# Re-timing six steps in a hand-ordered attention and feed-forward kernel: hash, turns, norm, means and loads

## The chip, the cores and the metric

The kernel runs on one core of one Trainium2 chip. The metric is device microseconds of one execution; of several runs the median is told. Engines are named as the profile names them: PE is TensorE (PEld its weight loads), DVE is VectorE, ACT is ScalarE, POOL is GpSimd and SP is SyncE, which here only issues DMAs.

## The reference

Inputs are q, k and v (4 batches, 8 heads, 768 tokens, 64 dims), a projection to 6 hash bits, and the weights of a gated feed-forward layer.

```
q_bucket, k_bucket = bits of (q @ proj > 0), (k @ proj > 0), read as numbers
scores = (q @ k.T) / 8, and -1e9 where the buckets differ
attn   = softmax(scores) @ v                       # per batch and head
x      = attn as [4 * 768 tokens, 8 * 64]
xn     = x / sqrt(mean(x * x) + 1e-6) * rms_g
out    = (silu(xn @ w_gate) * (xn @ w_val)) @ w_out    # 512 -> 1536 -> 512
```

## The kernel before, in words

The tokens are worked on in eight windows w of 384 queries: batch b = w // 2, half w % 2. A window has 8 heads, in 4 pairs hp. The attention of one head against all 768 keys is three slots, p = 0, 1, 2; a slot is one pair of score products (`scores`, L344) into one PSUM tile and one exponential on ACT over it (`probs`, L354). The mask is part of the score product: q and k carry 12 further rows of hash bits below their 64 dims, so the tile `QK` has 76 rows. Value products (`av`, L366) come two and three slots behind the head's last slot, in two halves of nine.

All order is written out by hand. `plan[s]` holds the steps of slot s, put there by `at(s, step, ..., rank=)`. The main loop takes slot after slot: first `scores(s + 1)`, then the steps of rank under 3, then `probs(s + 1)`, then the rest by rank. Each engine executes its instructions in this order, so a step that waits holds back all that stands behind it on the same engine.

The pieces that the change touches:

- Turns. In batch 0 and in the first pair of batch 1, q and k are turned on PE: `keep_pair(b, hp, i)` makes three transposes into a PSUM bank `t_ps` (L170) and has DVE copy them to `kT` or `qT` (L178), for i = 0 to 3: k and q of the pair's first head, then of its second. `casts` brings the copy to fp16 in `QK`, mostly on POOL (L186), one half in batch 0 on ACT (L184). In the other pairs DVE turns the blocks itself (`turn_dve`, L194, four steps for k and four for q) straight from the loaded tile, and POOL casts (L202).
- Hashes. `hash_one`, `hash_pair`, `hash_lone`, `hash_pairs` compute four fp32 products into `d_ps` (L210), DVE turns them to `bits` (L217), and copies on DVE (L250, L270) or DMAs on SP's queue (L248, L268, L285, L303) move the 12 rows each to where they belong in `QK`. `hash_lone` and the later form of `hash_pair` issue eight such DMAs.
- Means. `v_mean` multiplies by ones (L325, a bank `m_ps`) and DVE scales it to `cvb` (L328), which `attn_out` adds.
- Output of a pair: `attn_out` on DVE (L381, L386), POOL (L390) and the squares on POOL (L402); the last pair of window 0 is on DVE alone (L390, L397). `sumsq` (L406) reduces the squares on DVE.
- The norm: `norm` (L413 on DVE, L415 and L419 on POOL), `scale_x` (L424 on DVE, one of three chunks), `turn_x` (four transposes on PE, L431, and one product on DVE, L432, into `xnT`). Then the feed-forward block of the window starts: `gate` (L446, tanh on ACT L448), `value` (L456, on DVE L457 and L458) and `project` (L469, copied out on ACT L476 and stored through SP L478). For window w it starts at slot s0 = 24 w + 42. All these small products share three PSUM banks (`bank`), in the order of program and release.
- Loads. `load_rows` (L112) and `load_blocks` (L122, four DMAs) go to SP's queue; weights (`load_w`, `load_wo`) go to POOL's. SP issues in order, and it uses eight completion semaphores in turn, so a DMA waits until the eighth one before it has landed.

The slots run through the pairs in this order, six slots to a line, window 0 and 1 first:

```python
TURNS = [(0, 0), (1, 0), (0, 1), (0, 2), (0, 3), (1, 1), (1, 2), (1, 3)]
TURNS += [(w + 2, hp) for w, hp in TURNS]
SLOTS = [(w, 2 * hp + hh, p) for w, hp in TURNS for hh in range(2) for p in range(3)]
SLOTS += [(w, h, p) for w in range(4, 8) for h in range(H) for p in range(3)]
```

So window 0's last head ends in slot 29, pair 0 of batch 1 is first used in slot 48, pair 1 in 60, pair 2 in 66 and pair 3 in 72.

Of the kernel before, what the change touches and what calls it, by code (L numbers as in the profile page):

```python
# [37 lines left out]
LAST = {(w, h): g for g, (w, h, p) in enumerate(SLOTS) if p == 2}  # L38
# [6 lines left out]
def kernel(  # L45
# [530 lines left out]
    def at(s, f, *a, rank=3):  # L576
        plan[s].append((rank, len(plan[s]), lambda: f(*a)))
# [17 lines left out]
        at(1 + h, cast_half, 0, h, "q", 1)  # L595
        at(h, (bits0, bits1)[h], (nc.vector,), 3)

    for hp, turns, sv in ((1, (1, 2, 4, 5), 8), (2, (7, 8, 9, 10), 17), (3, (12, 13, 14, 15), 22)):
        for i, s in enumerate(turns):
            at(s, keep_pair, 0, hp, i)  # L600
            at(s + 1, casts, 0, hp, i)
        at(sv, v_prep, 0, hp)

    for h, s in ((2, 3), (3, 7)):
        at(s, hash_one, h)
        for t in range(3):
            at(s + 1 + t, lambda h=h, t=t: moves[h]((nc.vector,), t), rank=5)
    for hp, s, slots in ((2, 12, (13, 14, 15, 16)), (3, 17, (18, 19, 20, 21))):
        at(s, hash_pair, 0, hp)
        for i, s in enumerate(slots):  # L610
            at(s, lambda hp=hp, i=i: moves[0, hp](nc.vector, [divmod(i, 2)]), rank=5)
    for hp, s in enumerate((6, 16, 22, 29)):
        at(s, v_mean, 0, hp, 2, range(6))
    for i, (t, src) in enumerate(((wg, moe_w_gate), (wv, moe_w_val))):
        at(2 + 4 * i, load_w, t, src, 0, 768)
# [3 lines left out]

    for which, sl in zip("kqv", (9, 11, 15)):  # L620
        at(sl, load_rows, nc.sync, 1, 0, which)
    for i, sl in enumerate((23, 25, 27, 29)):
        at(sl, keep_pair, 1, 0, i)
        at(sl + 1, casts, 1, 0, i)
    at(31, hash_pair, 1, 0)
    at(27, v_prep, 1, 0)
    for h in range(2):
        at(41 + h, cast_half, 1, h, "q", 0)
# [4 lines left out]
    def in_row(loads, s, hash_slot=None):  # L633
        return loads, range(s, s + 8), (s + 4, s + 8, s + 9), hash_slot

    work = {
        (1, 1): in_row((21, 22, 32), 42, 51), (1, 2): in_row((32, 33, 37), 49, 58),
        (1, 3): in_row((38, 40, 44), 56, 65),
        (2, 0): in_row((53, 55, 58), 64), (2, 1): in_row((59, 62, 66), 72, 81),
        (2, 2): in_row((68, 71, 75), 81), (2, 3): in_row((78, 82, 86), 89, 98),  # L640
        (3, 0): in_row((90, 94, 98), 100), (3, 1): in_row((100, 104, 108), 110, 119),
        (3, 2): in_row((116, 120, 124), 126), (3, 3): in_row((126, 130, 134), 136, 145),
    }
    for (b, hp), (loads, turns, cast_slots, sh) in work.items():
# [12 lines left out]
        at(cast_slots[2], v_sum, b, hp)  # L657
        if b > 1 and hp % 2:
            at(48 * b + (17 if hp == 3 else -4), v_mean, b, hp - 1, 4)
    for hp, s in enumerate((48, 62, 69, 78)):  # L660
        at(s, v_mean, 1, hp, 2)

    gts, sqs = {}, {}
# [13 lines left out]

    for w in range(8):
        for h in range(H):
            end = LAST[w, h] + 3  # L680
            at(end - 1, av, w, h, 0, 9)
            at(end, av, w, h, 9, 18)
            if h % 2:
                at(end, o_step, w, h // 2, rank=4.5)
                if (w, h) != (0, 7):
                    late = 3 if h == 7 and w < 3 else 5 if (w, h) == (0, 5) else 4
                    at(end + late, s_step, w, h // 2, rank=5 if late != 5 else 4)
        s0 = 24 * w + 42
        n0 = {0: 9, 2: 7}.get(w, 11)
        at(s0 - n0, norm, w, rank=5)  # L690
        for c in range(3):
            at(s0 - {0: 5 - c // 2, 2: 6 - c}.get(w, 8 - c), scale_x, w, c, rank=5)
            xs = {0: (3, 2, 1), 2: (4, 2, 1)}.get(w, (5, 3, 1))
            at(s0 - xs[c], turn_x, w, c, rank=1)
        seen = set()
        for ft in range(NF):
            for f, s in ((g_step, s0 + 16 * ft // NF), (v_step, s0 + (32 * ft + 16) // (2 * NF))):
                at(s, f, w, ft, rank=4 if s in seen else 2)
                seen.add(s)
        for i in range(9 if w < 7 else 6):  # L700
            c, j = divmod(i, 3)
            at(s0 + 16 + i, project, w, c, 4 * j, 4 * j + 4, rank=1 if i == 8 else 3)
# [61 lines left out]
```

## Time and profile before

| | us |
|---|---|
| median of 3 runs | 336.01 (335.22 to 336.15) |
| the profiled execution | 334.87 |
| its span, first to last instruction | 333.1 |
| PE busy | 324.1 (97%) |
| DVE busy | 237.9 (71%) |
| ACT busy | 207.8 (62%) |
| POOL busy | 155.6 (47%) |
| mean granted PE clock | 0.999 |

The profile is of one execution; the time of that execution is 1.8 us above its span. In its views a row "start, length, engine, line, operation, out<-in, count" may merge several instructions, and the bracket behind it is the idle time of the engine ahead of it and what ended that wait. Of the chain of waits each row is start, length and what the chain went through.

### The profile page before, as it was taken

Reading aid. Unit: us, or ns where it says so; the run is one execution under the profiler, and the core shown is the slowest. Engines: PE = TensorE matmul, PEld = TensorE weight load, DVE = VectorE, ACT = ScalarE, POOL = GpSimd, SP = SyncE. Lnnn points to the kernel's source line nnn. Section 1 sums busy time; section 2 is a strip of 40 time slices with the busy share of each in tenths; the row PEclk is TensorE's granted clock in tenths of the full one; section 3 lists DMA queues with packets and bytes.
Section 4 is the critical chain, followed back from the end, with each engine's and each line's share of the span. In section 5 each row is a group of like instructions: output and inputs, shape, how many; then the busy total and the mean of one; then the engine's idle time right before and its main releaser. Section 6 shows DMA issues by size and latency. Waiting matters only on the chain.

```text
span 333.1 us, 7797 instructions
## 1 busy us (share of the span) xinstructions
PE 324.1 (97%) x2983; PEld 199.3 (60%) x2983; DVE 237.9 (71%) x532; ACT 207.8 (62%) x324; POOL 155.6 (47%) x230
## 2 busy tenths in 40 slices
PE   8999989999989999999999999999999999999995
PEld 6566666555556556565566656566666656655653
DVE  4789669998588976789577785967357753793860
ACT  3789887665566666657576766657666766422421
POOL 5888955587666665737644364643110311130000
PEclk9999999999999999999999999999999999999999
DMA  7999999887649528308240751000100001002002
GB/s 218 355 229 207 159 138 147 146 143 104 138 83 171 100 49 213 46 18 153 102 81 15 147 128 63 3 16 4 65 33 0 3 31 65 2 1 83 13 0 94
DMA packets 85972, 31.36 MB, mean 94 GB/s; under 512 B 71480, under 2 KB 82992, under 8 KB 85936
## 3 DMA queue, kind: packets, MB, share of 16 engines
q1 hardware_dynamic: 82000, 26.09, 34.3%
q0 software_dynamic: 3712, 4.72, 8.8%
q8 instruction: 23, 0.38, 0.5%
q14 instruction: 13, 0.11, 0.1%
q10 hardware_dynamic: 224, 0.07, 0.1%
HBM read 28.32 MB, written 6.29 MB: 104 GB/s over the span
## 4 chain that ended last, share of the span: by engine, by line
PE 83%; DVE 7%; DMA 4%; POOL 2%; ACT 1%; issue 1%; SPq 0%; DVEq 0%; POOLq 0%; ACTq 0%
PE y_ps L469 18%; PE v_ps L456 16%; PE s_ps L344 15%; PE g_ps L446 14%; PE o_ps L366 8%; PE d_ps L210 4%; PE s_ps L446 4%; DMA wo<-in_moe_w_out_dram 2%; DMA QK<-bits 2%; PE x_ps L431 1%; PE t_ps L170 1%; PE z_ps L337 1%; PE y_ps L721 1%; DVE t L457 1%; DVE otmp L381 1%
## 5 line engine op out<-in xcount | busy, mean ns | idle before, releaser
L354 ACT ACTIVATE psb<-s_ps 128x768 f16<-128x768 f32 x192 | 150.6, 809 | 29.6 <-PE s_ps L344 27.9
L344 PE MATMUL s_ps<-QK 76*128 76x384 f16 x384 | 93.6, 325 | 2.2 <-ACT psb L354 0.9
L456 PE MATMUL v_ps<-xnT,wv 128*128 128x384 f16 x384 | 78.1, 326 | 0.0
L469 PE MATMUL y_ps<-wo,ht 128*128 128x512 f16 x276 | 69.4, 379 | 0.1
L448 ACT ACTIVATE t<-g_ps 128x384 f32<-128x384 f32 x78 | 38.2, 490 | 46.3 <-PE g_ps L446 45.7
L366 PEld LDWEIGHTS <-psb 128*128 128x128 f16 x1152 | 52.2, 97 | 21.8 <-issue 3.7
L457 DVE SCALAR_TENSOR_TENSOR t<-t,g_ps 128x384 f32<-128x384 f32 x78 | 42.7, 547 | 31.0 <-ACT t L448 30.4
L446 PE MATMUL g_ps<-xnT,wg 128*128 128x384 f16 x312 | 63.4, 325 | 1.2 <-DVE xnT L432 0.6
L390 POOL TENSOR_TENSOR x<-otmp,rcp 128x384 f32<-128x384 f32 x31 | 25.9, 835 | 79.3 <-DVE rcp L386 78.8
L458 DVE SCALAR_TENSOR_TENSOR ht<-t,v_ps 128x384 f16<-128x384 f32 x96 | 53.2, 554 | 10.5 <-PE v_ps L456 1.1
L366 PE MATMUL o_ps<-vl,psb 128*128 128x65 f16 x1152 | 56.7, 193 | 0.0
L446 PEld LDWEIGHTS <-wg 128*128 128x128 f16 x384 | 36.0, 97 | 25.1 <-issue 1.7
L456 PEld LDWEIGHTS <-wv 128*128 128x128 f16 x384 | 36.2, 97 | 23.4 <-issue 0.3
L344 PEld LDWEIGHTS <-QK 76*128 76x128 f16 x384 | 31.4, 98 | 19.9 <-issue 6.8
L469 PEld LDWEIGHTS <-ht 128*128 128x128 f16 x276 | 25.8, 97 | 25.1 <-issue 1.6
L476 ACT COPY ysb<-y_ps 128x512 f32<-128x512 f32 x23 | 13.5, 586 | 25.3 <-PE y_ps L469 24.9
L402 POOL TENSOR_TENSOR sq<-x 128x384 f32<-128x384 f32 x31 | 25.7, 828 | 2.5
L202 POOL CAST QK<-qT 64x768 f16<-64x768 f32 x22 | 18.2, 827 | 18.0 <-DVE qT L194 17.3
L432 DVE TENSOR_TENSOR xnT<-x_ps,gcol 128x512 f16<-128x512 f16 x24 | 16.2, 681 | 14.2 <-PE x_ps L431 14.2
L381 DVE TENSOR_TENSOR otmp<-o_ps,cvb 128x390 f32<-128x390 f32 x32 | 17.9, 558 | 8.2 <-PE o_ps L366 8.1
L202 POOL CAST QK<-kT 64x768 f16<-64x768 f32 x22 | 18.2, 828 | 10.5 <-PE v_ps L456 4.0
L194 DVE STREAM_TRANSPOSE kT<-kL 128x192 f32<-128x192 f32 x44 | 22.1, 517 | 0.0
(80 smaller groups left out, 300.0 us busy)
## 6 DMA issues: line engine op xcount, KB each, us to landing
vL<-in_v_dram SPq DMA_DIRECT2D x16, 384.0 KB
out_dram<-ysb SPq DMA_DIRECT2D x23, 256.0 KB
kL<-in_k_dram SPq DMA_DIRECT2D x44, 96.0 KB
qL<-in_q_dram SPq DMA_DIRECT2D x44, 96.0 KB
kL<-in_k_dram SPq DMA_DIRECT2D x4, 384.0 KB
qL<-in_q_dram SPq DMA_DIRECT2D x4, 384.0 KB
wg<-in_moe_w_gate_dram POOLq DMA_DIRECT2D x2, 768.0 KB, 8.6
wv<-in_moe_w_val_dram POOLq DMA_DIRECT2D x2, 768.0 KB, 9.1
```

The lines of the kernel that those rows point to most:

```text
L202: nc.gpsimd.tensor_copy(QK[b, hp][0:64, hh, o : o + S], T0[b, hp, which][64 * hh : 64 * hh + 64, :])
L344: nc.tensor.matmul(ps[:, j, 0:HALF], k_cols(w // 2, h, 2 * p + j), q_cols(w, h), start=True, stop=True,)
L354: nc.scalar.activation(psb[w, h][:, p], sps.pop(g)[:, :, 0:HALF], AF.Exp, scale=ESCALE,)
L366: nc.tensor.matmul(o[:, c, hh, 0:65], psb[w, h][:, jt // 2, jt % 2, 128 * c : 128 * c + 128], vls[b % 2][:, h, v_chunk(b, h, jt), 0:65], s ...
L390: eng.tensor_mul(xd.rearrange("p c (h d) -> p c h d", h=2), tmp[:, :, :, 0:64], r.to_broadcast([128, 3, 2, 64]),)
L402: nc.gpsimd.tensor_mul(sq, xd, xd)
L446: nc.tensor.matmul(g, wg[:, kt, fs], xnT[w][:, kt], start=(kt == 0), stop=(kt == 3))
L448: nc.scalar.activation(t, g, AF.Tanh, scale=0.5)
L456: nc.tensor.matmul(vv, wv[:, kt, fs], xnT[w][:, kt], start=(kt == 0), stop=(kt == 3))
L457: nc.vector.scalar_tensor_tensor(out=t, in0=t, scalar=1.0, in1=g, op0=ALU.add, op1=ALU.mult)
L458: nc.vector.scalar_tensor_tensor(out=ht[w][:, ft], in0=t, scalar=0.5, in1=vv, op0=ALU.mult, op1=ALU.mult)
L469: nc.tensor.matmul(y, ht[w][:, ft, c * 128 : (c + 1) * 128], wo[:, ft, :], start=(ft == 0), stop=(ft == NF - 1),)
```

## The change

Six kinds of steps get other slots; no instruction is added or taken away.

- The turn of head 3's k goes from slot 4 to 3, its casts from 5 to 4; the hash of head 2 from slot 3 to 4, and its three DVE moves one slot on each.
- The mean of pair 3 of batch 0 goes from slot 29 to 30, those of pairs 1 and 2 of batch 1 from 62 to 60 and from 69 to 64.
- The four turns of batch 1's first pair go from slots 23, 25, 27, 29 to 20, 21, 24, 27, the casts with them; its hash from 31 to 33.
- Loads: k and q of (1, 2) from 32 and 33 to 34 and 35; v of (2, 0) from 58 to 59; k, q, v of (2, 1) from 59, 62, 66 to 66, 67, 68; of (2, 2) from 68, 71, 75 to 71, 74, 77.
- The value products of window 0's last head, and with them its output step, go one slot sooner, from 31 and 32 to 30 and 31.
- Window 0's norm goes from slot 33 to 31, its three scalings from 37, 37, 38 to 36, its three turns from 39, 40, 41 to 38, 39, 40.

```diff
-    for hp, turns, sv in ((1, (1, 2, 4, 5), 8), (2, (7, 8, 9, 10), 17), (3, (12, 13, 14, 15), 22)):
+    for hp, turns, sv in ((1, (1, 2, 3, 5), 8), (2, (7, 8, 9, 10), 17), (3, (12, 13, 14, 15), 22)):
...
-    for h, s in ((2, 3), (3, 7)):
+    for h, s in ((2, 4), (3, 7)):
         at(s, hash_one, h)
...
-    for hp, s in enumerate((6, 16, 22, 29)):
+    for hp, s in enumerate((6, 16, 22, 30)):
         at(s, v_mean, 0, hp, 2, range(6))
...
-    for i, sl in enumerate((23, 25, 27, 29)):
+    for i, sl in enumerate((20, 21, 24, 27)):
         at(sl, keep_pair, 1, 0, i)
         at(sl + 1, casts, 1, 0, i)
-    at(31, hash_pair, 1, 0)
+    at(33, hash_pair, 1, 0)
...
-        (1, 1): in_row((21, 22, 32), 42, 51), (1, 2): in_row((32, 33, 37), 49, 58),
+        (1, 1): in_row((21, 22, 32), 42, 51), (1, 2): in_row((34, 35, 37), 49, 58),
         (1, 3): in_row((38, 40, 44), 56, 65),
-        (2, 0): in_row((53, 55, 58), 64), (2, 1): in_row((59, 62, 66), 72, 81),
-        (2, 2): in_row((68, 71, 75), 81), (2, 3): in_row((78, 82, 86), 89, 98),
+        (2, 0): in_row((53, 55, 59), 64), (2, 1): in_row((66, 67, 68), 72, 81),
+        (2, 2): in_row((71, 74, 77), 81), (2, 3): in_row((78, 82, 86), 89, 98),
...
-    for hp, s in enumerate((48, 62, 69, 78)):
+    for hp, s in enumerate((48, 60, 64, 78)):
         at(s, v_mean, 1, hp, 2)
...
-            end = LAST[w, h] + 3
+            end = LAST[w, h] + (2 if (w, h) == (0, 7) else 3)
             at(end - 1, av, w, h, 0, 9)
             at(end, av, w, h, 9, 18)
...
-        n0 = {0: 9, 2: 7}.get(w, 11)
+        n0 = {0: 11, 2: 7}.get(w, 11)
         at(s0 - n0, norm, w, rank=5)
         for c in range(3):
-            at(s0 - {0: 5 - c // 2, 2: 6 - c}.get(w, 8 - c), scale_x, w, c, rank=5)
-            xs = {0: (3, 2, 1), 2: (4, 2, 1)}.get(w, (5, 3, 1))
+            at(s0 - {0: 6, 2: 6 - c}.get(w, 8 - c), scale_x, w, c, rank=5)
+            xs = {0: (4, 3, 2), 2: (4, 2, 1)}.get(w, (5, 3, 1))
             at(s0 - xs[c], turn_x, w, c, rank=1)
```

## The prediction

> **What bounds the kernel now.** I read the page first, then busy time by stretch, then the chain of waits, and last the order of time where the chain leaves TensorE.
>
> ```profile
> PE 324.1 (97%) x2983; PEld 199.3 (60%) x2983; DVE 237.9 (71%) x532; ACT 207.8 (62%) x324; POOL 155.6 (47%) x230
> ```
>
> TensorE is busy for 324.1 of 333.1 us. Its work is the same before and after, so the change can only move the 9.0 us in which it is idle, or add to them.
>
> ```profile
> 10.00:15.00 5.00, 4.35 (x41) 2.55 (x40) 3.88 (x8) 3.97 (x6) 4.63 (x8) 1.00 1.07 382
> ...
> 25.00:30.00 5.00, 4.58 (x57) 2.79 (x55) 4.71 (x12) 4.38 (x8) 4.67 (x9) 1.00 1.12 228
> ...
> 90.00:100.00 10.00, 9.14 (x86) 5.66 (x85) 8.88 (x21) 6.53 (x11) 5.31 (x7) 1.00 0.49 103
> ```
>
> After the width stand PE, PEld, DVE, ACT and POOL busy, the granted clock (1.00, so it plays no part), the DMA engines' share and GB/s. TensorE's idle time lies ahead of the first feed-forward block (0.65 and 0.42 us in the two short rows, for instance) and once more at 90 to 100 us (0.86 us). In the early rows the DMA share is over 1: transfers queue there.
>
> **Part 1: head 2's hash a slot on, with the turn of head 3's k put ahead of it.**
>
> ```profile
> 11.54 0.49 PE L344 MATMUL s_ps<-QK 76*128 76x384 f16 x2
> ...
> 12.30 0.55 DVE L178 COPY qT<-t_ps 128x384 f32<-128x384 f32 x1
> ...
> 14.62 0.49 PE L344 MATMUL s_ps<-QK 76*128 76x384 f16 x2
> ```
>
> ```profile
> 12.44 1.31 PE d_ps L210 x8
> ...
> 14.18 0.33 PE t_ps L170 x3
> 14.51 0.27 PE o_ps L366 x9
> ...
> 39.05 0.85 PE d_ps L210 x8
> ```
>
> The hash matrix products cost 0.85 us undisturbed (39.05) and 1.31 us here, because they stand in TensorE's queue ahead of the copy of qT, which ends at 12.85. Scores(4) end at 12.0, so TensorE has little to do from there to 12.85. After the change the turn (0.33) and scores(5) (the same length in the chain's terms) fill that hole; the hash still ends at 12.85 + 0.85 = 13.70; the first half of a value product (0.27) follows, and scores(6) start at 13.97 in place of 14.62: 0.65 sooner. The three DVE moves of head 2's bits come a slot later; their users, scores(12), are six slots off, so they cost nothing. The other end is zero, if DVE gets to the signs later because of the extra copy (0.56) queued ahead; that copy fits between 12.85 and 13.7, so I take 0.6.
>
> **What keeps that 0.6 from reaching the end.**
>
> ```profile
> 29.15 4.38 DMA QK<-bits
> 33.58 0.66 PE s_ps L344 x3
> ...
> 40.52 0.54 DVE ssp L406
> ...
> 42.38 0.74 DVE sq L397 x6
> ...
> 43.77 0.90 POOL rstd L419
> ...
> 44.69 0.89 DVE xn L424 x2
> ...
> 46.64 1.80 DVE xnT L432 x3
> ...
> 48.49 0.65 PE g_ps L446 x3
> ```
>
> Scores(25), at 33.58, wait for a bit row of pair 3 that took 4.38 us from its issue. With the DMA engines at shares of 1.07 and 1.12, I read this as a backlog that ends at about 33.5 whenever the small transfer is issued. Then the 0.6 is lost there. The Trainium skill points the other way ("DMA: Bandwidth & Descriptors", "Queues, rings and completion order"): each DMA engine goes round the queue rows packet by packet and takes one row's descriptors in order, so a row issued sooner should land sooner even with a weight load of POOL's in flight. That is the second rival below.
>
> **Part 2: batch 1's first pair turned sooner and hashed in 33, head 7's values and the first norm sooner.**
>
> ```profile
> 33.95 4.40 ACT L354 ACTIVATE psb<-s_ps 128x768 f16<-128x768 f32 x6 [0.34 <-PE s_ps L344]
> 34.24 0.83 POOL L310 CAST vl<-vL 128x768 f16<-128x768 f32 x1
> 35.01 1.07 POOL L186 CAST QK<-kT 64x384 f16<-64x384 f32 x2
> 36.57 0.43 PE L366 MATMUL o_ps<-vl,psb 128*128 128x65 f16 x9
> 37.53 0.82 POOL L402 TENSOR_TENSOR sq<-x 128x384 f32<-128x384 f32 x1
> 38.23 0.81 PE L344 MATMUL s_ps<-QK 76*128 76x384 f16 x4
> 40.37 0.44 PE L366 MATMUL o_ps<-vl,psb 128*128 128x65 f16 x9
> ```
>
> Slots advance at ScalarE's pace here, 4.40 / 6 = 0.73 us. From 33.6 to scores(32) the new order holds two turns and the mean where the old one held three turns and the mean; at ScalarE's pace that is worth little, so I leave scores(32), the second pair of the 38.23 row, at about 38.6. The second half of head 7's value product then follows in that slot, at 38.9; before, the hash (0.85) and a further slot stood between, and it ran at 40.37. That is 1.4 us sooner. The norm cannot use it all. DVE's reduction of pair 2's squares stands ahead of head 7's output step, and POOL makes those squares later: 1.07 us of casts now precede them, and pair 1's step, from which POOL's work follows, comes about 0.2 sooner (the 0.6 of Part 1 less one turn, 0.33), so the 37.53 square ends at about 39.2 in place of 38.35. From there: reduction 0.54, output step 1.3 (40.52 + 0.54 to 42.38), squares 0.74, sum and its neighbours to rstd's end 1.55 (43.12 to 44.67), xn 1.34 (three at 0.45), an output step of the next pair about 0.7, xnT 1.80. Sum 7.97, from 39.2: 47.2. TensorE itself gets there later: from scores(32) at 38.6 two slots (1.4), the slot with the hash (0.7 + 0.85 less what ScalarE's pace hides, 1.3), eight slots of 0.73 (5.8) and a pair of scores (0.4) make 47.5. Gate at about 47.6 for 48.49: 0.9 sooner. Ends: 0.3, when POOL's chain is 1.0 later, and 1.5, when the bits land 0.6 sooner.
>
> Three covers in this part. POOL's cast of pair 3's values (34.24) now stands behind the 1.07 us of casts and ends at about 36.0; its user, the product at 36.57, then comes at about 36.0 to 36.3: covered by 0 to 0.3, and up to 0.3 lost if POOL slips. The 2 copies that DVE takes in slots 20 and 21 fall in its fullest row (4.71 of 5) and can delay pair 1's output step by 0.56; with the next cover that makes the lower end. The mean of pair 3, a slot on, is used by the output step right behind it, which POOL's squares hold back anyway.
>
> ```profile
> L270 DVE COPY QK<-bits x8: 251/279/777, 24.8 to 31.9; 12x384 f16<-12x384 f16 x8
> ```
>
> These moves of bits run among the new copies; one took 777 ns where the median is 279. The Trainium skill has a rule for that ("SBUF — State Buffer", "Who interferes with whom"): a DVE copy in a two-port mode and a GpSimd instruction exclude each other for a whole instruction. The spread here agrees with it. By it the sum below would be 0.8 in place of 1.3, because two such moves run among POOL's new casts (0.5 more for one of them); I keep to the median.
>
> **Part 3: loads of (2, 1) and (2, 2) later, means sooner.**
>
> ```profile
> 94.43 0.81 PE L446 MATMUL g_ps<-xnT,wg 128*128 128x384 f16 x4 [0.47 <-DVE t L457]
> 96.56 0.48 PE L344 MATMUL s_ps<-QK 76*128 76x384 f16 x2 [0.39 <-DMA QK<-bits]
> 85.89 2.85 SPq L122 DMA_DIRECT2D kL<-in_k_dram  x4
> 89.47 2.67 SPq L122 DMA_DIRECT2D qL<-in_q_dram  x4
> 92.91 7.05 SPq L285 DMA_DIRECT2D QK<-bits  x8
> 99.47 0.54 DVE L194 STREAM_TRANSPOSE kT<-kL 128x192 f32<-128x192 f32 x1
> 100.25 0.54 DVE L457 SCALAR_TENSOR_TENSOR t<-t,g_ps 128x384 f32<-128x384 f32 x1
> 102.21 0.81 PE L456 MATMUL v_ps<-xnT,wv 128*128 128x384 f16 x4
> ```
>
> ```profile
> 94.59 1.84 DMA QK<-bits
> ```
>
> The two waits (0.39 + 0.47) are the 0.86 us at 90 to 100. The first is SP's: the 8 bit transfers of the pair (1, 3) stand behind the loads of (2, 1), whose 8 issues take 2.85 + 2.67 = 5.5 us. They now stand ahead and go 5.5 us sooner. The second is a PSUM bank held by a mean, which moves to slot 64 and gives the gate an older bank. Both go: 0.86, less perhaps 0.15 in slot 64, where the moved mean makes a project wait for an xnT. Net 0.7.
>
> What is late next is the load of k for (2, 1). The bits start at 92.91 - 5.7 = 87.2; eight of them take 6.2 (7.05 has one long last one), an output of a finished block 0.6, and three of the four k issues 2.1: the last k issue starts at about 96.1. DVE turns it in slot 72, and in DVE's queue the reduction and t of the next value step stand behind that wait, for whose bank v_ps at 102.21 waits. The landing takes at least 1.84 (the bits, 94.59) and at most 4.38 (bits in a full queue). At the start of the kernel
>
> ```profile
> 0.72 0.40 SPq L114 DMA_DIRECT2D kL<-in_k_dram  x1
> 3.89 0.55 PEld L170 LDWEIGHTS t_ps<-ident,kL 128*128 128x128 f32 x3
> ```
>
> a k load is used 3.2 us after its issue; the queue is as empty at 96, so I take 3.2: landed at 99.3. DVE would come to it at 99.47 - 0.9 - 0.7 = 97.9, and waits 1.4. From that turn to the end of t is 100.79 - 99.47 = 1.32, so t ends at 100.6; v_ps wants it at 102.21 - 1.6 = 100.6. No loss yet, but DVE, at 8.88 of 10, has little room to catch up: I charge 0.3. The other moved loads cost nothing: those of (1, 2) go a slot or two on and are turned from slot 49, those of (2, 2) up to three slots on, to 77, and are turned from 81. v of (1, 1) now goes ahead of the 8 bits of (1, 0):
>
> ```profile
> 43.64 6.66 SPq L268 DMA_DIRECT2D QK<-bits  x6
> ...
> 55.82 0.49 PE L344 MATMUL s_ps<-QK 76*128 76x384 f16 x2
> ```
>
> the last of them goes out at 50.3, and scores(48) at 55.82 use the first three. One more transfer ahead and 0.9 less time leave over 3 us.
>
> **Sum.** 0.9 + 0.7 - 0.3 = 1.3 us. The profiled execution took 334.87 us, 1.8 more than its span; it would take 333.6, the span 331.8. The median of the runs is 336.01: 334.7 us.
>
> **The rivals.** A measurement of this kernel tells 0.3%, 1.0 us, from no change.
> First, given back: the first gate takes its lower end. Gain 0.3 + 0.7 - 0.3 = 0.7, 335.3 us, and with v's cast and the late load at 0.5 each worse down to a loss of 0.3 to 0.5, 336.5. For it: the 4.67 of 5 for POOL and 4.71 for DVE. Against: the 1.4 us by which head 7's value product moves. Chance 0.24.
> Second, the bits land sooner by the 0.6 of Part 1, because a small transfer does not sit out the whole backlog: then the gate starts at 47.0, 1.5 sooner, and the sum is 1.9 with the same charges: 334.1 us. (The Trainium skill's queue rule, quoted above from "DMA: Bandwidth & Descriptors", gives this case.) For it: the bits took 1.84 us in the quieter queue at 94.59. Against: the share of 1.12. Chance 0.15.
> Third, slower: the load of k for (2, 1) decides. Every microsecond by which it lands after 99.3 is one that DVE, and behind it TensorE, loses; from 100.6 on the gain is gone, and from 101.6 on the kernel is over 0.3% slower, at 337.0 and up (landing 5.5 us after the issue, or SP 2.3 us late). Against: DMA share only 0.49 there. For: SP issues without a pause from 85.89 to 100. Chance 0.18.
>
> **Numbers.** Forecast as worked out 0.43, faster 0.43 + 0.15 = 0.58, same 0.24, slower 0.18. The range runs from Part 2 at its upper end with Part 3 uncharged (1.5 + 0.86 = 2.36, 333.65, and 0.25 for the spread of runs, 335.22 to 336.15) at 333.4 to the edge of the first rival at 336.5; about a fifth is left out, most of it the slower case.
>
> **What would show it.** Right: hash of head 2 ending near 13.7 with scores(6) at 14.0; scores(25) still at 33.5; the first gate near 47.6; no wait for bits before scores(72); DVE idle ahead of a kT turn near 98 for about 1.4 us. Wrong: the first gate at 48.3 or later, or v_ps of slot 74 waiting on t for over 1 us.

## The result and the profile after

The changed kernel takes 334.80 us in the median of 15 runs (333.92 to 335.63), the one before 336.01 (335.22 to 339.58). The ratio is 0.9948, interval 0.9927 to 0.9969. Timed again on another chip it was 334.68 against 335.54: 0.9966, interval 0.9941 to 0.9991. Both intervals lie below 1: the changed kernel is faster by 0.9 to 1.2 us between the medians, and the two intervals together leave 0.3 to 2.5 us open. The forecast was 334.7. Here and below medians are over all runs and ratios over those in the fast state, so a ratio need not be the quotient of the two medians beside it.

The profile taken with it does not show this at first sight: 335.63 us, span 333.8, longer than the 333.1 of the profile before. It is the longest of the 15 runs; the profiled one before was shorter than all 15 of its own. How TensorE is busy in the changed kernel, by stretch (columns as before), and below it two of these stretches in the kernel before:

```profile
PE 324.9 (97%) x2983; PEld 199.9 (60%) x2983; DVE 237.3 (71%) x532; ACT 208.1 (62%) x324; POOL 155.7 (47%) x230
```

```profile
10.00:15.00 5.00, 4.75 (x45) 2.99 (x45) 4.30 (x9) 4.27 (x7) 3.92 (x8) 1.00 1.07 377
...
30.00:35.00 5.00, 3.46 (x48) 2.73 (x47) 3.77 (x9) 4.00 (x6) 3.26 (x5) 1.00 0.73 172
...
90.00:100.00 10.00, 10.00 (x92) 6.43 (x91) 8.49 (x19) 7.76 (x14) 4.81 (x6) 1.00 0.50 106
100.00:110.00 10.00, 9.53 (x88) 5.90 (x86) 8.45 (x20) 6.10 (x10) 6.06 (x9) 1.00 0.94 165
```

```profile
30.00:35.00 5.00, 4.63 (x62) 3.45 (x61) 4.31 (x10) 4.48 (x7) 3.91 (x5) 1.00 0.65 151
...
100.00:110.00 10.00, 9.91 (x99) 6.46 (x98) 8.51 (x21) 6.43 (x12) 5.56 (x8) 1.00 0.93 183
```

Idle time at 10 to 15 us fell from 0.65 to 0.25, and the 0.86 us at 90 to 100 are gone; 0.47 is idle at 100 to 110 (0.09 before), and 1.54 at 30 to 35 (0.37 before). The waits of TensorE name the causes (total, times, longest):

```profile
PE s_ps L344 <- DMA QK<-bits: 1.5, 1, 1.5
...
PE v_ps L456 <- DVE t L457: 0.5, 1, 0.5
PE y_ps L469 <- DMA wo<-in_moe_w_out_dram: 0.3, 1, 0.3
```

From the order of time:

```profile
4.64 0.85 PE L170 MATMUL t_ps<-ident,qL 128*128 128x128 f32 x3
...
8.73 0.48 PE L344 MATMUL s_ps<-QK 76*128 76x384 f16 x2 [0.21 <-ACT qT L178]
...
14.75 0.49 PE L344 MATMUL s_ps<-QK 76*128 76x384 f16 x2
```

The first scores start at 8.73 us, 0.77 later than before, in a stretch that the change does not touch: TensorE still ran at half speed there (three transposing products took 0.85 us; the same three took 0.49 before, at 4.55; the column of the granted clock, 1.00, does not show this). So early places are compared from here on by their distance from the first scores. Scores(6) start 14.75 - 8.73 = 6.02 us after them; before, 14.62 - 7.96 = 6.66.

From the chain of waits of the changed kernel:

```profile
13.54 0.99 PE d_ps L210 x8
...
29.46 5.72 DMA QK<-bits
35.22 0.34 PE s_ps L344
...
49.05 0.77 PE g_ps L446 x4
```

Head 2's hash ends at 14.53. The first bit row of pair 3 took 5.72 us from its issue (4.38 before), and scores(25) waited 1.5 us for it; the list of waits before has none of that size. The first gate starts at 49.05, 40.3 after the first scores; before, 48.49 - 7.96 = 40.5. From the order of time around the moved load:

```profile
94.64 2.71 SPq L122 DMA_DIRECT2D kL<-in_k_dram  x4
...
96.34 0.49 PE L344 MATMUL s_ps<-QK 76*128 76x384 f16 x2
...
100.99 0.54 DVE L194 STREAM_TRANSPOSE kT<-kL 128x192 f32<-128x192 f32 x1 [1.59 <-DMA kL<-in_k_dram]
...
102.37 0.81 PE L456 MATMUL v_ps<-xnT,wv 128*128 128x384 f16 x4 [0.45 <-DVE t L457]
```

Scores(72) at 96.34 wait for nothing. DVE stands 1.59 us for the load of k, and v_ps loses 0.45 behind it.

### The profile page after: what moved, and what is told of

Read it like the earlier page. It is cut to its first block, busy times and chain, and to the rows that moved or that the text cites. A ratio compares the mean times of both kernels' runs of the same rounds, so it can differ in the third digit from the quotient of the medians.

```text
span 333.8 us, 7798 instructions
## 1 busy us (share of the span) xinstructions
PE 324.9 (97%) x2983; PEld 199.9 (60%) x2983; DVE 237.3 (71%) x532; ACT 208.1 (62%) x324; POOL 155.7 (47%) x230
## 4 chain that ended last, share of the span: by engine, by line
PE 85%; DMA 5%; DVE 4%; ACT 2%; POOL 2%; issue 1%; SPq 1%; DVEq 0%; POOLq 0%; ACTq 0%
PE y_ps L469 18%; PE v_ps L456 17%; PE s_ps L344 16%; PE g_ps L446 13%; PE o_ps L366 9%; PE d_ps L210 4%; PE s_ps L446 4%; DMA wo<-in_moe_w_out_dram 2%; DMA QK<-bits 2%; PE x_ps L431 2%; ACT psb L354 1%; PE t_ps L170 1%; DMA kL<-in_k_dram 1%; PE z_ps L337 1%; PE y_ps L721 1%
## 5 line engine op out<-in xcount | busy, mean ns | idle before, releaser
L446 PEld LDWEIGHTS <-wg 128*128 128x128 f16 x384 | 36.0, 97 | 23.9 <-issue 0.4
L344 PEld LDWEIGHTS <-QK 76*128 76x128 f16 x384 | 31.5, 98 | 20.0 <-issue 4.8
L202 POOL CAST QK<-qT 64x768 f16<-64x768 f32 x22 | 18.2, 827 | 17.3 <-DVE qT L194 16.5
L202 POOL CAST QK<-kT 64x768 f16<-64x768 f32 x22 | 18.2, 828 | 10.7 <-PE v_ps L456 4.0
```

Of the source, the lines that this page charges most:

```text
L202: nc.gpsimd.tensor_copy(QK[b, hp][0:64, hh, o : o + S], T0[b, hp, which][64 * hh : 64 * hh + 64, :])
L344: nc.tensor.matmul(ps[:, j, 0:HALF], k_cols(w // 2, h, 2 * p + j), q_cols(w, h), start=True, stop=True,)
L446: nc.tensor.matmul(g, wg[:, kt, fs], xnT[w][:, kt], start=(kt == 0), stop=(kt == 3))
```

## The experiments

**Each part alone, and the changed kernel again.** The edits on the kernel before:

```diff
# part1_only
-    for hp, turns, sv in ((1, (1, 2, 4, 5), 8), ...
+    for hp, turns, sv in ((1, (1, 2, 3, 5), 8), ...
-    for h, s in ((2, 3), (3, 7)):
+    for h, s in ((2, 4), (3, 7)):
# part2_only: the means (.., 29) -> (.., 30), turns (23, 25, 27, 29) -> (20, 21, 24, 27),
#   the hash 31 -> 33, loads of (1, 2) (32, 33, 37) -> (34, 35, 37), and the lines of av, norm, scale_x, turn_x
# part3_only
-        (2, 0): in_row((53, 55, 58), 64), (2, 1): in_row((59, 62, 66), 72, 81),
-        (2, 2): in_row((68, 71, 75), 81), ...
+        (2, 0): in_row((53, 55, 59), 64), (2, 1): in_row((66, 67, 68), 72, 81),
+        (2, 2): in_row((71, 74, 77), 81), ...
-    for hp, s in enumerate((48, 62, 69, 78)):
+    for hp, s in enumerate((48, 60, 64, 78)):
```

> The kernel before with only head 2's hash a slot on and the last turn of pair 1's but one a slot sooner. Forecast's theory: scores(6) 0.65 us sooner counted from the first scores (6.0 in place of 6.66), lost again where scores(25) wait for the bits of pair 3; time 336.0, the same as before. Rival 'bits land sooner': scores(25) 0.4 to 0.6 sooner, counted from the first scores 25.0 in place of 25.18 plus the wait, the gate 0.6 sooner, 335.4.

> The kernel before with only batch 1's first pair turned in slots 20, 21, 24, 27 and hashed in 33, the mean of pair 3 in slot 30, head 7's values and the first norm sooner, and the loads of (1, 2) in 34, 35, 37. Forecast's theory: first gate 0.9 us sooner, counted from the first scores 39.6 us in place of 40.53, time 335.1. Rival 'nothing': the gate comes at 40.3 to 40.5 after the first scores and the time is 336.0.

> The kernel before with only the moved loads of (2, 0), (2, 1), (2, 2) and the two means of pairs 1 and 2 of batch 1. Forecast's theory: this part carries 0.86 - 0.15 - 0.3 = 0.4 us, so 335.6 for a before of 336.0, and the two waits at 90 to 100 us (0.47 on t, 0.39 on the bits) are gone, with 0.3 to 0.5 us of a new wait on t near 102. Rival 'all of it': parts 1 and 2 bring nothing, since the first feed-forward block starts no sooner when counted from the first scores (40.32 us after them in the changed kernel, 40.53 in the one before); then this part alone gives the whole measured 1.2 us or more, 334.8.

> The changed kernel once more, for a second profile. In the first one TensorE ran its first matrix products at half speed up to about 6.6 us (0.42 us a transposing product where the kernel before had 0.27 from 4.5 us on), the first scores came at 8.73 in place of 7.96, and the bits of pair 3 landed at 35.2 in place of 33.5. If both are chance of that execution: first scores at about 8.0, no wait of 1.5 us before scores(25), the first gate at 47.6 (39.6 after the first scores), time 334.8. If they are the change's own doing: the same 8.7, 35.2 and 49.0 again.

Measured on one chip, before at 335.54:

| kernel | median us | ratio, interval | first gate after first scores |
|---|---|---|---|
| part 1 | 335.39 | 0.9996 (0.9963 to 1.0029) | 40.29 |
| part 2 | 335.54 | 0.9999 (0.9976 to 1.0022) | 40.39 |
| part 3 | 335.27 | 0.9997 (0.9968 to 1.0026) | 40.20 |
| changed | 334.68 | 0.9966 (0.9941 to 0.9991) | 39.87 |

No part alone can be told from no change by its time, and the intervals leave room for a gain of 0.8 to 1.2 us each; the places in the traces tell more. Two lines of the waits in part 2's trace, and one in part 3's:

```profile
PE y_ps L469 <- DMA wo<-in_moe_w_out_dram: 2.4, 1, 2.4
...
PE g_ps L446 <- DVE t L457: 0.5, 1, 0.5
```

```profile
PE v_ps L456 <- DVE t L457: 0.3, 1, 0.3
```

Part 1 alone has scores(6) at 6.01, as forecast, and no time from it. Part 3 alone loses the bank's wait and gets the forecast wait on t. Parts 1 and 2, each alone, bring the gate forward little or not at all. They are not independent: POOL's squares of pair 2 end 32.36 us after the first scores with part 2 alone and 31.84 with part 1 as well (both traces of the changed kernel), so part 1's gain does reach the norm once part 2 is in. And a wait that no forecast priced shows up: the output product for the second half of wo. In the changed kernel's second trace:

```profile
68.50 0.94 POOL L526 DMA_DIRECT2D wo<-in_moe_w_out_dram  x1
...
75.62 0.59 PE L469 MATMUL y_ps<-wo,ht 128*128 128x512 f16 x2
78.45 0.59 PE L469 MATMUL y_ps<-wo,ht 128*128 128x512 f16 x2 [2.23 <-DMA wo<-in_moe_w_out_dram]
```

From issue to landing this load took 7.8 to 8.0 us in four executions and 9.9 to 10.1 in two (part 2 alone and this one). TensorE waits at most 0.34 us for it, or over 2. The same load stands in the kernel before, so this is likely a part of the spread of its runs too; its one trace does not show it.

**The load of wo sooner by three slots.** On the kernel before, on the changed one, and there with two more edits:

```diff
-        at(31 + 21 * i, load_wo, 6 * i, 6 * i + 6)
+        at(31 + 18 * i, load_wo, 6 * i, 6 * i + 6)      # all four
-    for i, sl in enumerate((20, 21, 24, 27)):
+    for i, sl in enumerate((20, 21, 24, 29)):           # cast_late, cast_kturn
-        (2, 1): in_row((66, 67, 68), 72, 81),
+        (2, 1): ((66, 67, 68), range(73, 81), (77, 81, 81), 81),   # cast_kturn
```

> The kernel before with the load of wo's second half issued in slot 49 in place of 52. In the profiles so far this load took 7.8 to 8.0 us from its issue at about 68.5 us in four executions and 9.9 to 10.1 in two, and the output product that needs it waited 0.2 to 0.35 us or 2.2 to 2.4. Theory 'a lottery behind the gate': issued about 8 us sooner it lands before its user in both cases; the wait is gone, the time falls by 0.2 us where the load is quick and by 2.2 where it is slow, so 335.2 for a before of 335.6 to 336.0, with fewer runs above 336.5. Rival 'moved contention': the load collides with the loads of (1, 2) and (1, 3) and TensorE waits for those instead; time the same or up to 1 us longer.

> The changed kernel with the same sooner load of wo's second half. With that lottery gone, what the change itself is worth stands out against before_wo_early on this chip. Forecast's sum: 1.3 us below it. From the profiles so far: the first gate 0.2 to 0.6 sooner, part 3 0.64, so 0.8 to 1.2 below it, at about 334.2. Rival 'the gain was luck': 0.3 or less below it.

> As changed_wo_early, and the last turn of batch 1's first pair in slot 29 in place of 27, so that POOL's two casts of it (1.05 us) stand behind pair 2's output and squares in place of ahead of them. Theory 'POOL's casts ate part 2': the squares of pair 2 end about 1.0 us sooner, counted from the first scores 30.8 in place of 31.8, and the first gate comes 0.4 to 0.6 sooner, at 39.4 in place of 39.9, where TensorE's own work limits it; time 0.5 below changed_wo_early. Rival 'DVE's order decides': the reduction and the output step of pair 3 stand behind a copy of the moved turn and behind the mean, and the gate does not move.

> As changed_wo_cast_late, and the turns of (2, 1) one slot later each (73 to 80 in place of 72 to 79, casts in 77 and 81), so that DVE comes to the first of them when its load has landed. Forecast's theory: the charge of 0.3 us in part 3 (measured 0.45 in one profile of the changed kernel, 0.3 in part 3 alone) comes back, no wait on t near 102 us; time 0.3 below changed_wo_cast_late. Rival: the wait of 1.6 us on DVE was covered, or the later casts of (2, 1) are late for the hash in slot 81; the same time or 0.5 longer.

Measured against 335.64: 340.06 (1.0138, interval 1.0105 to 1.0171), 338.41 (1.0075), 338.05 (1.0072), 338.77 (1.0055). My theory fell: the wait on wo is gone, but the kernel is 4.4 us longer, where the rival's contention was priced at 1 us at most. The waits, one stretch and the order of time of the first:

```profile
PE s_ps L344 <- DMA QK<-bits: 6.6, 3, 2.9
```

```profile
100.00:110.00 10.00, 7.86 (x64) 4.45 (x61) 5.64 (x12) 4.35 (x8) 4.45 (x7) 0.83 0.41 112
```

```profile
57.74 0.94 POOL L526 DMA_DIRECT2D wo<-in_moe_w_out_dram  x1
61.21 2.12 SPq L112 DMA_DIRECT2D vL<-in_v_dram  x1
63.43 5.20 SPq L122 DMA_DIRECT2D kL<-in_k_dram  x4
...
73.26 6.20 SPq L285 DMA_DIRECT2D QK<-bits  x8
```

The load of q that SP issued at 57.76, just behind POOL's, landed its first piece at 65.2, behind the weight load's first at 64.4. SP's next issues wait for landings: the load of v that goes out at 56.64 before goes out at 61.21, the four issues of k behind it take 5.20 us in place of 4.45 (from 57.32 in the trace before), and the bits of (1, 1), issued from 65.65 before, go out at 73.26.

Not all of the 4.4 us is waiting. In the stretch shown the granted clock is 0.83, so 1.7 of its 10 us are lost to the clock; TensorE had just waited 2.1 us there for bits. The traces of changed_wo_early and cast_kturn show such a loss of 1.7 us too (clock 0.85 and 0.90 at 80 to 90, 0.98 and 0.93 at 90 to 100), beside waits for bits of 2.5 and 2.6 us. No other trace has one before its last two microseconds, though two of them wait 2.2 and 2.4 us for wo, and the wait of 2.9 us in the first trace passed without. All six runs of before_wo_early have a mean granted clock of 0.990 to 0.995, where 28 of the 29 runs before on this chip have 0.998 or more; by 0.006 of 335 us the clock is worth an estimated 2 us of the 4.4.

This also blurs the other three, whose runs are a mixture: 8, 5 and 8 of 12 are at 0.990 to 0.995. The changed kernel is still below the one before on the common ground of the moved load, by 1.65 us in the medians (338.41 to 340.06) and by 1.3 if only its eight runs at such a clock are taken (338.78). The cast and the k turn brought nothing to be seen here. In the trace of cast_late the squares of pair 2 end at 40.65, 32.4 after the first scores, no sooner: the casts ahead of pair 2's output belong to the third turn, in slot 24, not to the fourth that I had moved.

**The right casts, and the load of wo sooner by one slot.**

```diff
# changed_casts_behind
-    for i, sl in enumerate((20, 21, 24, 27)):
+    for i, sl in enumerate((20, 21, 26, 27)):
# changed_wo_slot51
-        at(31 + 21 * i, load_wo, 6 * i, 6 * i + 6)
+        at(31 + 20 * i, load_wo, 6 * i, 6 * i + 6)
```

> The changed kernel with the third turn of batch 1's first pair in slot 26 in place of 24, so that POOL's casts of it (1.05 us) stand behind pair 2's output and squares. (The run with the last turn in slot 29 left these casts where they were: the ones ahead of the output are those of the third turn.) Theory 'POOL's casts ate part 2': the squares of pair 2 end 1.0 us sooner, counted from the first scores 30.8 in place of 31.8, the output step of pair 3 starts at 31.4 in place of 32.35, and the first gate comes at 39.3 to 39.5 in place of 39.9 to 40.3, TensorE's own work being the limit from there; time 0.5 to 0.8 below the changed kernel, 334.0 to 334.3. Rival 'the same POOL work comes back later': the casts then delay the casts and weight load behind them, head 7's values or the norm's steps on POOL, and the gate stays at 39.9 to 40.3.

> The changed kernel with the load of wo's second half one slot sooner (51 in place of 52), which puts it ahead of the cast and the three sums of pair (1, 1)'s values in POOL's queue: 2.8 us sooner, at about 65.7. Eight microseconds sooner cost 4 us, since eleven loads of SP's queue landed only behind it; here the same queue holds the bits of (1, 1), which scores(60) need at 75.2. Theory 'its own latency': lands at 73.5 to 75.8, ahead of its user at 76.2 in nearly all executions; the wait (0.34 and 2.2 in the two profiles of the changed kernel) is gone and no other takes its place; 0.3 to 1.0 below the changed kernel, no run above 336. Rival 'it holds up the bits': the bits of (1, 1) land behind it, at 73.5 to 76, and scores(60) wait up to 1 us; no gain, or up to 1 us longer.

Measured against 335.47: 334.54 (0.9966, interval 0.9944 to 0.9987) and 334.30 (0.9972, interval 0.9951 to 0.9992). POOL's work and its users first in the changed kernel (second trace, first scores at 8.75), then with the casts behind (first scores at 7.86):

```profile
35.16 1.08 POOL L186 CAST QK<-kT 64x384 f16<-64x384 f32 x2
...
36.30 0.82 POOL L310 CAST vl<-vL 128x768 f16<-128x768 f32 x1
37.18 0.43 PE L366 MATMUL o_ps<-vl,psb 128*128 128x65 f16 x9 [0.30 <-POOL vl L310]
37.19 0.50 POOL L186 CAST QK<-qT 64x384 f16<-64x384 f32 x1
37.74 1.05 POOL L186 CAST QK<-kT 64x384 f16<-64x384 f32 x2
38.87 0.82 POOL L390 TENSOR_TENSOR x<-otmp,rcp 128x384 f32<-128x384 f32 x1
39.77 0.82 POOL L402 TENSOR_TENSOR sq<-x 128x384 f32<-128x384 f32 x1
...
40.63 0.56 DVE L406 TENSOR_REDUCE ssp<-sq 128x3 f32<-128x384 f32 x1 [1.41 <-POOL sq L402]
41.10 0.55 DVE L381 TENSOR_TENSOR otmp<-o_ps,cvb 128x390 f32<-128x390 f32 x1
...
48.62 0.81 PE L446 MATMUL g_ps<-xnT,wg 128*128 128x384 f16 x4
```

```profile
36.50 0.51 POOL L186 CAST QK<-qT 64x384 f16<-64x384 f32 x1
...
37.09 0.82 POOL L390 TENSOR_TENSOR x<-otmp,rcp 128x384 f32<-128x384 f32 x1
38.00 0.82 POOL L402 TENSOR_TENSOR sq<-x 128x384 f32<-128x384 f32 x1
38.77 1.06 POOL L186 CAST QK<-kT 64x384 f16<-64x384 f32 x2
...
39.36 0.56 DVE L381 TENSOR_TENSOR otmp<-o_ps,cvb 128x390 f32<-128x390 f32 x1
...
47.46 0.81 PE L446 MATMUL g_ps<-xnT,wg 128*128 128x384 f16 x4
```

POOL goes from one instruction to the next with hardly a gap, and DVE's reduction waits 1.41 us for it. With 1.05 us of casts behind, the squares end 30.96 after the first scores in place of 31.84, the output step starts at 31.5 in place of 32.35, and the gate at 39.60 in place of 39.87. The casts held up the output step; of the 0.85 us that it gains, 0.3 reach the gate (39.87 in the changed kernel's trace shown; in its other one, where the bits of pair 3 were late, it is 40.27), since TensorE and ScalarE's pace are next: the chain of waits from 33 us to the gate runs over these two alone. The time of this kernel cannot be told from the changed kernel's.

With the load in slot 51, from the order of time:

```profile
65.40 0.94 POOL L526 DMA_DIRECT2D wo<-in_moe_w_out_dram  x1
...
75.32 1.03 PE L469 MATMUL y_ps<-wo,ht 128*128 128x512 f16 x4
```

It landed at 73.4, the product ran without a wait, and no scores waited for the bits. One run in 12 was above 336 (336.49); I had said none.

**Both together, and the turns of (2, 1) a slot later.** The same two edits, and for the second kernel the k turn edit shown above.

> The changed kernel with both mends: POOL's casts behind pair 2's output (third turn in slot 26) and wo's second half loaded in slot 51. Each alone gave about 334.4 (334.54 and 334.3 against 335.47 before); the first gate came at 39.6 after the first scores with the one, and no output product waited for wo with the other. If the two are independent: gate at 39.6, no wait on wo, time 0.3 to 0.6 below either, 333.8 to 334.1 for a before of 335.5. Rival 'one hides the other': with the casts moved POOL reaches the load sooner by itself (67.34 in place of 68.5 us in that profile), so the second mend adds nothing, 334.3 to 334.5.

> As changed_both_mends, and the turns of (2, 1) one slot later each (73 to 80, casts in 77 and 81). Forecast's charge of part 3: a wait on t of 0.3 to 0.5 near 102 us where the load of k lands late; in the last two profiles there was none. Theory: 0 to 0.3 below changed_both_mends. Rival: the hash of slot 81 and what hangs on it come later, 0.3 above.

Measured against 335.61: 333.78 (0.9955, interval 0.9926 to 0.9984) and 334.54 (0.9972, interval 0.9945 to 0.9998). The first has the lowest median of all, at the lower edge of the 333.8 to 334.1 forecast, but on another chip than the changed kernel; its ratio lies between the two of the changed kernel (0.9948 and 0.9966), so that it beats it is not shown. Its profiled execution, one of its longer ones at 335.85, shows the price of part 3 at its worst:

```profile
101.25 0.53 DVE L194 STREAM_TRANSPOSE kT<-kL 128x192 f32<-128x192 f32 x1 [2.49 <-DMA kL<-in_k_dram]
102.62 0.81 PE L456 MATMUL v_ps<-xnT,wv 128*128 128x384 f16 x4 [1.34 <-DVE t L457]
```

It also waits 0.73 us, at 75.21, for a cast of POOL's (L202), which no other trace does. With the turns a slot later (kturn) the wait on t is gone, and two others stand in the list of that trace:

```profile
PE s_ps L344 <- DMA QK<-bits: 1.6, 1, 1.6
...
PE x_ps L431 <- DVE xn L424: 0.8, 1, 0.8
```

The first is that of scores(25) once more, far ahead of the edit. The second costs more than the 0.3 that the rival was priced at: from scores(84) to scores(108) both traces with this edit need 39.64 us, all eight others with part 3 38.67 or 38.68. The eight turns pushed into later slots stand in DVE's queue ahead of the next norm's scaling; that it is they that hold it up was not tried by itself.

## Why the prediction was right, and where it was not

The time (334.7 for 334.80) and the direction were right. Two terms of the sum were too large, so that the time was hit to 0.1 us is in part luck; the second measurement, 0.86 us between the medians, lies further from the forecast 1.3.

**Part 1, right.** Scores(6) were forecast 0.65 us sooner and came 0.64 to 0.65 sooner in every trace that has the edit; the hash ended 5.80 after the first scores (5.74 forecast). That part 1 by itself is lost at scores(25) was right too, and the traces say more of where. In 13 of 14 executions the first bit row of pair 3 landed 0.4 to 1.4 us behind the last piece of POOL's load of wg, whatever its own issue: issued at 29.15 and landed at 33.5 with wg at 32.7; issued at 29.46 and landed at 35.2 with wg at 34.1. By the Trainium skill ("DMA: Bandwidth & Descriptors", "Queues, rings and completion order") each DMA engine goes round the queue rows packet by packet, by which a small transfer should overtake the weight load. The second rival stood on this; here the first of its pieces land early (1.2 us after the issue) and the last ones behind the weight load, and its user waits for the last. No run moved that weight load, so that it is the cause is not tested. The forecast landing at 33.5, whatever the issue, held in twelve of the 14 (33.0 to 33.9) and not in the first of the changed kernel and one more (35.2).

**Part 2, wrong in size: forecast 0.9, 0.2 to 0.4 measured.** The gate comes 40.1 us after the first scores in the mean of the five traces with this part as it is (39.87 to 40.39) and 40.3 in the four without (40.20 to 40.53). In the two with part 1 and no wait for bits up to scores(25) it is 39.87 and 39.92. My own sign for a failure, a first gate at 48.3 or later, came true in both traces of the changed kernel (49.05 and 48.62, of which 0.8 is the later start). The step that failed is the end of pair 2's squares: forecast 39.2 us, 31.24 after the first scores, measured 31.84. I let pair 1's step come 0.2 sooner; it came 0.1 later (POOL's output 23.9 after the first scores in place of 23.75), since DVE copies the new turn (0.56 at 31.16) ahead of it. That was named as an end of the range and not taken. And POOL's casts cost their 1.05 us and 0.26 of pauses between its instructions, which the sum left out. The longer moves of bits that the prediction priced at 0.5 and set aside did not come: one of eight took 0.78 us before and after. The rest of the chain held where no bits were late: from the squares' end to the gate 7.97 were forecast, and 48.62 - 40.59 = 8.03 measured; so did TensorE's own way, forecast at 39.5 and seen at 39.6 once the casts were out of it. The cover of the cast of pair 3's values also failed as priced: 0.30 us at 37.18.

**Part 3, its gain right and one charge missing: 0.4 net forecast, 0.2 measured.** Both waits went. From scores(66) to scores(84) five traces with this part need 30.84 us in the mean (30.62 to 31.12), the three without, with the load of wo where it was, 31.54 (31.45 to 31.69): 0.7 gained, the wait on t included. But part 3 also costs TensorE twice. From scores(61) to scores(66) the five need 0.22 us more (7.51 to 7.53 for 7.29 or 7.30); the forecast charged 0.15 there. And from scores(89) to scores(90) all ten traces with part 3 need 1.98 us, all four without 1.70: a project waits until ACT has copied an earlier one out. The lists of waits do not have it; the chain of waits of part 3 alone does:

```profile
122.78 0.59 ACT ysb L476
...
123.41 1.02 PE y_ps L469 x4
```

So these 0.28 us were put at nothing. The moved means change which of the three banks each later product gets, which fits such a wait; that it is they and not the moved loads was not tried. The net from scores(61) to scores(108) is 77.03 us in place of 77.23. The late load of k was foreseen in place and size: issued last at 96.72 (forecast 96.1), DVE idle 1.59 (1.4), v_ps waiting 0.45 (0.3). (In the working the bits go out 5.7 us sooner where its two rows add up to 5.5; nothing hangs on it.) The 1.3 to 1.5 us of the third rival's mechanism appeared in two executions of other versions, changed_both_mends (32.00 us from scores(66) to scores(84), not among the five) and cast_late; there part 3 loses more than it gains.

**The sum.** 0.2 to 0.4 and 0.2 make 0.4 to 0.6 us by the traces, where 1.3 were forecast and the medians give 0.9 to 1.2. The quickest of 125 runs before took 334.31 us, the quickest of 27 of the changed kernel 333.88, which is 0.43 and agrees with the traces. What the medians show beyond that stays open: landings that vary from one execution to the next (bits, k, wo) are as large, and one trace for each run cannot tell how often each comes. So the mechanism of the first rival, a gate at its lower end (0.3), is what the traces show in part 2, and the forecast of the time came out nearer than its terms. Set against its own profiled time, 334.87, the forecast span of 331.8 was not seen in either trace of this kernel (333.8, 334.8), each of which carried a late start and a wait on a transfer; the quickest run had 332.1.

## What to carry to other kernels

Compare a single profile with another only from a common event behind the start, and look first for waits on loads whose landing varies: here they are as large as the whole gain. Moving a step sooner pays only if the engines that serve it have room: 1.05 us of casts ahead of POOL's output cost 0.9 at its squares and 0.3 at the gate. A price can also stand far behind the edit and in no list of waits, as the 0.28 us at scores(89) do; compare the distance between two fixed events stretch by stretch. A bulk load on another queue is not free because it is early: see whose landings it holds up, where their bits are needed, and whether the wait costs clock as well.

## What was not expected of the hardware

By the length of its products, TensorE changed from half to full speed at about 4.4 us (before) and between 6.6 and 6.9 us (changed) after the start of kernels that are the same up to there. The first scores came between 7.86 and 8.82 us over the traces, in one of them (8.75) partly because of a wait of 0.56 us for DVE. The Trainium skill ("TensorE: Matmul & The Clock Gate", "Part 1: The HAM clock gate") gives a free-running window as the reason and about 4 us of matrix products, give or take half a microsecond. From the first product at 1.04 us it is 3.4 and about 5.7 us here: more than twice the spread that the page gives.

Later in the kernel the granted clock fell in three traces, for a loss of 1.7 us each, around waits of 2.1 to 2.6 us for bits; waits of 2.2 and 2.4 us for wo and one of 2.9 us for bits passed without.

Transfers that SP issued while a weight load of POOL's was in flight landed their last pieces behind it: 0.4 to 1.4 us behind in 13 of 14 executions for the first bit row of pair 3. The weight load's own landing varied too: wo's second half took 8.0 and 9.9 us from its issue in two executions of the same kernel.
